# Two heads per matmul in the block means of the first batch, a wider first mixing product, a split last product, and a new order of all steps

## The chip, the cores and the metric

The kernel runs on one core of a Trainium2 chip. The metric is device time in microseconds. Before the change three runs took 621.28, 622.59 and 622.96 us; the median, 622.59 us, is the number to compare with. One more execution was taken with the hardware profiler: it took 626.52 us, and its trace spans 624.3 us from the first to the last instruction.

## What is computed

Per batch (4 batches, 8 heads of 64 dimensions, 768 positions) a local attention of window 16 that also sees 24 block summaries, and then a feed-forward layer of width 2048 on the 512 joined channels, with a low-rank mixing over positions in front of it. Cut to what matters here:

```python
k_sum = k.reshape(B, H, nb, block, D).max(axis=3)        # block = 32, nb = 24
v_sum = v.reshape(B, H, nb, block, D).mean(axis=3)
scores_all = concat([where(mask_l, q @ k.T / 8, -1e9), q @ k_sum.T / 8 + log(32)])
x = softmax(scores_all) @ concat([v, v_sum])             # heads joined: (B, S, 512)
u = x + (x.T @ U @ V).T                                  # U: (768, 32), V: (32, 768)
out = u + relu(u @ w_ch1) @ w_ch2                        # (512, 2048), (2048, 512)
```

## The kernel before

Everything is written as small steps with short names, and a table, `PLAN`, lists the steps in the order in which they are recorded; each engine carries its own instructions out in that order. The part up to the first slash is the attention of batch 0 and its way into the feed-forward layer (names with a leading dot); every later slash is a place between two groups of products of the layer, into which steps of later batches are put. Nothing else sets the order, so a step that waits holds all that stands behind it on its engine.

**Batch 0** is called the head here. Its steps are: loads of keys, queries and value pairs (`.lk`, `.lq`, `.lv`, lines 310, 324, 345, all on SP's queue, each waiting until the load eight places ahead of it has landed), block maxima and their spreading (`.K`, `.Kp`, `.Kd`, lines 418 and 433), scores (`.S`, line 474), mask and exponentials on DVE and ACT (`.E`, lines 499 and 509), transposes (`.T`, line 583), copies of them (`.C`, line 589), the product with the values (`.V`, line 599), the normalising (`.N`, line 629). Block means of the values are made by TensorE: `block_means` (`.M0`, `.M1`, line 399) multiplies a 32-column selection matrix with the values of one head, 65 columns with the column of ones. Four heads go to the four groups of 32 output partitions, and the loop over the heads is the inner one, so that matmuls next to each other write to different groups: 48 matmuls for four heads. `block_means_out` (`.Mo`, line 411) copies the result to `vsum`, and `value_summaries` (`.Bp`, `.Dp`, ..., line 437) puts it into each head's values, which `.V` reads.

The mixing of batch 0 is `mix_t` (`.I`, line 642; two tiles of 128 channels at a time), `mix_s` (`.J`, line 660) and `mix_u` (`.G`, lines 676 and 684: three transposes and the product that adds the mixed rows). Then come the products of the feed-forward layer, `up` (line 1015, 12 matmuls of 384 columns) and `down_rows` (line 1037, nine of 512) in turn. Matmuls of no use (`keep_busy`, `.w4`, line 1139, four of 120 columns each) stand where TensorE would have nothing to do.

**Batches 1 to 3** have their attention spread over the products of the batch before. Batch 3 ends with `second_phase` (line 1498): sums of products of 384 columns, each added to the rows that are kept (line 1524) and sent (line 1529).

Float32 matmuls show as two records in the trace, each with a weight load; the products of the layer show as one.

Of the kernel before, what the change touches and what calls it, by code (L numbers as in the profile page):

```python
# [18 lines left out]
P = 128  # L19
# [16 lines left out]
VALS = 8  # L36
# [31 lines left out]
    .lu .li .X .w4 .z1 .w4 .lk0 .lk3 .K0 .Xt0 .Kd0 .lq0 .lm .lq3 .lk2 .K3 .S0 .Kd3 .S3 .m .K2  # L68
    .Kp2 .E0.2 .w4 .lq2 .E0.1 .lk1 .F .w4 .lq1 .E1.0 .E7.0 .E6.2 .E1.1 .lv0 .S2 .lv1 .E0.0 .E1.2
    .T1 .K1 .E7.2 .Xt1 .T0 .E7.1 .C0 .E6.1 .lk7 .C1 .E5.2 .E5.0 .E6.0 .Kp1 .E5.1 .lk6 .w4 .T7  # L70
    .S1 .T5 .Xt2 .E2.0 .E4.1 .E2.1 .lq7 .T6 .E3.0 .lq6 .lq4 .M0 .E3.2 .E2.2 .E3.1 .Mo0 .Dp0
    .E4.0 .lk4 .K7 .Kp7 .lk5 .T2 .Bp1 .T3 .C6 .E4.2 .C5 .K6 .Bp0 .C7 .S7 .Kd6 .V1 .C2 .lv2 .T4
    .Dp3 .Xs .Bp3 .V0 .V7 .K4 .E15.2 .lq5 .Kp4 .Dp2 .E14.2 .E15.1 .V6 .C3 .N3 .E15.0 .E14.1 .lv3
    .S6 .Xl .C4 .la0 .S4 .K5 .Qs .E14.0 .Bd2 .Dp1 .E8.1 .V5 .E13.0 l1.0.0 .Kp5 .V4 .E8.2 .N0 .S5
    .E12.2 .E8.0 .V3 .V2 .E11.1 .E13.1 .E12.0 .M1 .lr .E9.0 .E12.1 .E11.2 .T12 .E13.2 .E11.0
    .E9.1 .T8 .T15 .Mo1 .Z0 .C12 .C15 .Dp6 .E10.2 .E10.1 .la1 .Qf .E10.0 .N1 .N2 .T13 .lb0 .T14
    .I0 .Y0.0 .T11 .E9.2 .Bd6 .Dd5 .T9 .Io0 .C11 .Bp4 .Bp7 .C13 .la2 .C8 .Y0.1 .Dp4 .V12 .lb1
    .C9 .V11 .V13 .Y0.2 .J0 .lb2 .V8 .N6 .la4 .Bp5 .T10 a1.0.0 .la3 .V9 .C14 .V14 .Jo0 .C10 q1.0
    .V10 .Dp7 .N4 k1.0 .G0.0 .V15 .G0.1 .lb3 .N5 .Z1 .N7 .Go0.0 a1.0.0 .G1.1 .Go0.1 .I2 .G1.0
    .Y1.0 .Io2 .J2 .z0 .w4 .Y1.1 .Jo2 .G0.2 .W0 .G0.3 .Y1.2 .Go0.2 l1.0.1 .Go0.3 .Z2 .G1.2  # L80
    .Go1.1 .Go1.2 a1.0.0 t2 W0.5 .G1.3 a1.0.0 .Go1.0 t2 .Go1.3 .U0.0 .W1 a1.0.0 / / / t2 c0.4 t2
    t2 a1.0.0 K1.0 .lb4 t2 c0.3 t3 a1.0.0 a1.0.1 w0.0 c1.2 / l1.1.0 w0.1 / x1.1 t3 x0.2 t3 v1.1
    D1 Ka1.0 v1.0 / c1.3 k1.1 S1.0.1 / E1.0.1.0 E1.0.1.1 W0.6 E1.0.1.2 S1.0.0 t3 a1.0.1 t4
    E1.0.0.1 t3 c0.5 E1.0.0.0 D0 K1.1 t5 a1.0.1 E1.0.0.2 a1.0.1 t3 Ka1.1 x0.3 w1.0 / T1.0 x1.2
    q1.1 k1.2 K1.2 / / c1.4 S1.1.0 a1.0.1 t4 / E1.1.0.2 W1.5 U0 S1.1.1 E1.1.0.0 a1.1.0 E1.1.0.1
    W1.6 s1.0 Ka1.2 q1.2 U1 w1.1 E1.1.1.2 E1.1.1.0 t4 a1.0.1 D2 E1.1.1.1 t4 k1.3 Us0 t4 t4 t5 t5
    Us1 f1.0 / c1.5 U4 a1.0.1 a1.0.1 x1.3 / D3 x0.4 a1.0.1 c0.6 / W0.7 t6 S1.2.0 t5 Ba1.1.1 U3
    T1.1 W0.8 E1.2.0.1 Ba1.0.0 E1.2.0.0 a1.1.0 E1.2.0.2 / t5 s1.1 t5 / q1.3 x0.5 W1.7 t6 x1.4
    a1.1.0 D4 S1.2.1 W0.9 Ba1.0.1 E1.2.1.1 K1.3 f1.1 E1.2.1.2 / E1.2.1.0 t6 / t6 c0.7 c0.8 P1.0
    Ba1.1.0 t6 / c1.6 W1.8 N1.0 T1.2 w2.0 t7 Ka1.3 t8 k1.4 / S1.3.0 / s1.2 E1.3.0.2 E1.3.0.0  # L90
    S1.3.1 t6 E1.3.0.1 q1.4 c1.7 P1.1 w2.1 k1.5 x1.5 E1.3.1.0 E1.3.1.1 t7 v1.2 E1.3.1.2 N1.1
# [36 lines left out]
    q2.6 E2.5.0.1 f2.3 h1.2 / / F P2.3 R2.0 K2.6 a2.1.1 / / d1.1 v2.4 p0 p1 K2.7 a2.1.1 q2.7 p1
    h1.3 s2.4 Kd2.6 / / a2.1.1 F y1.2 / E2.5.1.2 p0 d2.0 p1 p0 / E2.5.1.1 / N2.3 / / R2.1
    Ba2.4.1 Ba2.4.0 F Ds0 E2.5.1.0 Ds1 / v2.5 h1.4 f2.4 / / k3.0 y1.3 p1 S2.6 T2.5 s2.5 p0  # L130
    E2.6.1.1 E2.6.0.1 / / p0 E2.6.1.2 / r2.1 E2.6.0.0 Kd2.7 E2.6.1.0 / E2.6.0.2 a3.0.0 h1.5 r2.0
    p1 Ba2.5.1 / y1.4 K3.0 P2.4 d3.0 f2.5 v2.6 M2.0 d2.1 / N2.4 Mo2.0 / / y1.5 d3.1 T2.6 h1.6 /
    p0 / / / F a3.0.0 / S2.7 / Ba2.5.0 E2.7.0.0 E2.7.0.2 E2.7.1.0 Ba2.6.0 E2.7.1.1 g2.0 E2.7.1.2
    / / y1.6 d4.0 / / E2.7.0.1 / d4.1 / J2.0 Jo2.0 s2.6 P2.5 / p1 h1.7 Ds2 T2.7 g2.1 y1.7 /
    a3.0.0 / F k3.2 / Ds4 h1.8 p0 d5.0 p0 O2.0.1 N2.5 O2.0.1 p0 v2.7 / d5.1 K3.2 f2.6 y1.8 / F
    Ds5 O2.0.2 / O2.0.0 h1.9 / Ba2.6.1 / / y1.9 / F / / O2.0.2 h1.10 / p1 Kd3.2 O2.0.1 R2.2 /
    d7.0 P2.6 Ba2.7.0 a3.0.0 l3.0.1 s2.7 / / / p0 Kd3.0 r2.2 / / p1 / / p1 y1.10 / O2.0.3 / / p0
    p0 d6.0 h1.11 y1.11 d6.1 q3.0 Ba2.7.1 O2.0.1 h1.12 p1 / f2.7 / / / a3.0.1 P2.7 a3.0.0 O2.0.2
    / y1.12 O2.0.1 / / N2.6 / p1 O2.0.3 N2.7 p1 R2.3 Ds3 p0 M2.2 O2.0.1 O2.0.2 / / / / d7.1 g2.2
    h1.13 / / Mo2.2 O2.0.3 J2.2 O2.0.3 O2.0.3 p0 O2.0.2 O2.0.2 / / y1.13 F p1 Ds6 p0 r2.3 a3.0.1  # L140
# [50 lines left out]
def body(ctx: ExitStack, tc, q0, q1, k, v, vn, uv, w1, w2, mask, ident, rep, out):  # L191
# [1290 lines left out]
    def second_phase(st):  # L1482

        banks = {}
        for i in range(8 * len(OPS)):
# [20 lines left out]
            if q == 3:  # L1506
                second_out(st, i, n, c, ps)
# [157 lines left out]
```

## Time and profile before

| | |
|---|---|
| median of 3 runs | 622.59 us |
| profiled execution, its own time | 626.52 us |
| its span | 624.3 us |
| TensorE busy | 610.4 us (98%) |
| VectorE, ScalarE, GpSimd busy | 446.5, 350.9, 345.6 us |
| SP's DMA queue | 147.38 MB |

TensorE is the engine to look at: it is busy for nearly all of the span. The granted clock column shows 1.00 in every stretch but the last. What remains is to see where TensorE waits, and which of its work is needed.

### The profile page before, as it was taken

The numbers are of one execution on the slowest core, as the hardware profiler recorded it, in microseconds if no ns is written. First come the engines' busy times: TensorE is split into PE (matmuls) and PEld (weight loads), VectorE is DVE, ScalarE is ACT, GpSimd is POOL, SyncE is SP. The second block draws the span as 40 slices with busy tenths as digits, with TensorE's granted clock in tenths as the row PEclk, the third lists the DMA queues.
The fourth block names the chain that finished last, engine by engine and source line by source line (L and its number), as shares of the span: only waits on it lengthen the run. The fifth ranks groups of instructions, "written<-read, shape, count | busy, mean of one in ns | idle before, by whom it ended". The sixth has DMA issues, their size and how long they took to land.

```text
span 624.3 us, 14694 instructions
## 1 busy us (share of the span) xinstructions
PE 610.4 (98%) x5376; PEld 557.9 (89%) x5376; DVE 446.5 (72%) x1139; ACT 350.9 (56%) x794; POOL 345.6 (55%) x393
## 2 busy tenths in 40 slices
PE   7899999999999999999999999999999999999997
PEld 6679989889987999988887899998888899999997
DVE  5689768678888766779787764776557553579992
ACT  3776666563653666665544556675463556767620
POOL 5377964786666687785345677654333575640000
PEclk9999999999999999999999999999999999999999
DMA  8997998999968678799896786687879645455443
GB/s 222 230 323 246 285 313 258 288 291 325 295 197 281 226 239 262 241 301 300 262 305 181 210 266 203 198 256 237 253 242 311 220 133 168 149 191 203 145 119 126
DMA packets 97559, 148.30 MB, mean 238 GB/s; under 512 B 9680, under 2 KB 67920, under 8 KB 97488
## 3 DMA queue, kind: packets, MB, share of 16 engines
q1 hardware_dynamic: 97488, 147.38, 76.4%
q8 instruction: 42, 0.69, 0.5%
q14 instruction: 29, 0.24, 0.1%
HBM read 104.67 MB, written 42.66 MB: 236 GB/s over the span
## 4 chain that ended last, share of the span: by engine, by line
PE 81%; DMA 12%; SPq 3%; DVE 1%; issue 1%; ACT 1%; POOL 1%; DVEq 0%; ACTq 0%
PE ps_h L1300 25%; PE acc L1396 17%; PE ps_h L1015 10%; PE acc L1037 10%; PE accx L1498 4%; PE accy L1498 3%; PE accz L1498 3%; DMA place<-in_k 2%; PE ps_x L613 2%; DMA dsum<-tmp 2%; PE ps_s L474 2%; PE ps_s L451 2%; DMA there<-squares 2%; SPq L542 1%; DMA whole<-up 1%; DMA place<-in_v 1%
## 5 line engine op out<-in xcount | busy, mean ns | idle before, releaser
L967 POOL TENSOR_TENSOR parts<-whole,parts 128x512 fp32r<-128x512 f32 (+1 forms) x128 | 159.3, 1258 | 77.3 <-ACT parts L963 72.9
L1300 PE MATMUL ps_h<-place,parts 128*128 128x384 f32 x1008 | 179.5, 336 | 0.7 <-DVE x L629 0.7
L1300 PEld LDWEIGHTS ps_h<-place,parts 128*128 128x128 f32 x1008 | 174.3, 188 | 3.0 <-PE ps_h L1300 1.0
L1396 PE MATMUL acc<-gh,parts 128*128 128x256 f32 (+1 forms) x512 | 133.6, 341 | 0.0
L1396 PEld LDWEIGHTS acc<-gh,parts 128*128 128x128 f32 x512 | 88.6, 189 | 12.3 <-issue 1.4
L963 ACT CAST parts<-whole 128x512 fp32r<-128x512 f32 (+1 forms) x144 | 80.8, 581 | 11.9 <-issue 4.6
L1396 PE MATMUL acc<-gl,parts 128*128 128x512 f32 (+1 forms) x256 | 86.5, 338 | 0.0
L1015 PE MATMUL ps_h<-place 128*128 128x384 f32 x384 | 73.9, 341 | 0.4 <-DVE x L695 0.3
L509 ACT ACTIVATE e<-e,neg 128x120 f32<-128x120 f32 x144 | 52.0, 390 | 33.4 <-DVE neg L499 32.3
L1015 PEld LDWEIGHTS ps_h<-place 128*128 128x128 f32 x384 | 67.2, 188 | 3.1 <-DVE x L695 0.7
L1037 PE MATMUL acc<-place,gh 128*128 128x512 f32 x192 | 66.5, 400 | 0.0
L1369 ACT ACTIVATE gh<-place 128x768 fp32r<-128x768 f32 x32 | 27.1, 846 | 62.2 <-PE acc L1396 62.2
L264 POOL TENSOR_SCALAR val<-place 128x512 f32<-128x512 f32 (+1 forms) x33 | 54.1, 1642 | 9.4 <-ACT place L244 4.4
L289 POOL TENSOR_TENSOR place<-val,place 128x512 fp32r<-128x512 f32 x29 | 37.6, 1301 | 29.7 <-ACT place L288 25.2
L1374 DVE SCALAR_TENSOR_TENSOR gl<-place,gh 128x768 fp32r<-128x768 f32 x32 | 38.3, 1196 | 20.3 <-ACT gh L1369 20.2
L1396 PEld LDWEIGHTS acc<-gl,parts 128*128 128x128 f32 x256 | 48.5, 189 | 4.5 <-DVE gl L1374 0.2
L743 POOL TENSOR_TENSOR place<-tmp,place 128x384 fp32r<-128x384 f32 x24 | 27.8, 1163 | 41.0 <-ACT place L739 34.2
L1037 PEld LDWEIGHTS acc<-place,gh 128*128 128x128 f32 x192 | 36.1, 188 | 7.4 <-ACT gh L1027 0.2
L499 DVE CUSTOM_DVE_ANT_0 e<-ps_s,mask_sb 128x120 f32<-128x120 f32 x144 | 35.1, 276 | 6.2 <-PE ps_s L451 4.1
L1027 ACT ACTIVATE gh<-ps_h 128x384 fp32r<-128x384 f32 x32 | 15.7, 489 | 41.0 <-PE ps_h L1015 40.9
L1037 PE MATMUL acc<-place,gl 128*128 128x512 f32 x96 | 37.7, 393 | 0.0
L1329 DVE TENSOR_TENSOR place<-place,ps_h 128x384 f32<-128x384 f32 x24 | 13.3, 554 | 28.7 <-PE ps_h L1300 28.6
(153 smaller groups left out, 1043.4 us busy)
## 6 DMA issues: line engine op xcount, KB each, us to landing
place<-in_w SPq DMA_DIRECT2D x32, 512.0 KB, 5.8
whole<-up SPq DMA_DIRECT2D x24, 512.0 KB, 4.8
there<-squares SPq DMA_DIRECT2D x24, 384.0 KB, 4.8
at<-there SPq DMA_DIRECT2D x96, 96.0 KB, 3.4
whole<-up SPq DMA_DIRECT2D x24, 384.0 KB, 3.9
whole<-down SPq DMA_DIRECT2D x16, 512.0 KB, 5.6
vt<-in_v SPq DMA_DIRECT2D x48, 146.2 KB, 4.2
kt<-in_k SPq DMA_DIRECT2D x24, 288.0 KB, 4.8
```

The lines of the kernel that those rows point to most:

```text
L264: nc.gpsimd.tensor_scalar(f32(bits), f32(hi), 0.0, None, ALU.mult)
L289: engine.tensor_tensor(lo, val, f32(hi), ALU.subtract)
L499: nc.vector.tensor_tensor_reduce(out=e[:, u, :], in0=ps[:, i * KC : (i + 1) * KC], in1=mask_sb[:, m, :], scale=-SCALE, scalar=BIG, op0=ALU ...
L509: nc.scalar.activation(e[:, u, :], e[:, u, :], AF.Exp, bias=st.neg[h][:, u : u + 1], scale=-1.0,)
L963: nc.scalar.copy(hi, whole)
L967: (nc.vector if key[0] == "second" else nc.gpsimd).tensor_tensor(lo, whole, f32(hi), ALU.subtract)
L1015: nc.tensor.matmul(ps[:, :NH], w_split[0, f][:, c % 2, part_w, c // 2], ut[c], start=(n == 0), stop=(n == 3 * NC - 1),)
L1037: nc.tensor.matmul(acc[t], gt[:, sl], w_split[1, f][:, part_w], start=(first and j == 0), stop=(last and j == 2),)
L1300: nc.tensor.matmul(ps, a[:, sa, i], b[i][:, sb], start=(first and n == 0), stop=(n == 5), skip_group_check=not first,)
L1374: nc.vector.scalar_tensor_tensor(gl, h, 0.0, f32(gh), ALU.max, ALU.subtract)
L1396: nc.tensor.matmul(place, w[:, part_w, c * P : (c + 1) * P], gt[:, q0:q1], start=(f == 0 and i == 0 and j == 0), stop=(f == NF - 1 and j = ...
L1498: nc.tensor.matmul(ps, w[j][:, sa, c * P : (c + 1) * P], gate[sb], start=fresh and q == 0 and j == 0 and k == 0, stop=q == 3 and j == 1 an ...
```

## The change

- `block_means` takes two heads per matmul: 130 columns in place of 65, 24 matmuls for four heads, in two steps (`.M0.0`, `.M0.1`). Each step fills one group of 32 output partitions with 12 matmuls in a row; groups 2 and 3 are not used. `block_means_out` copies the two halves one after the other.
- `mix_t` of batch 0 mixes 256 channels per matmul where it does two tiles at once, and the channel tiles 2 and 3 are now mixed one by one (`.i2`, `.i3`, `.j2`, `.j3`).
- `mix_u` of batch 0 is taken apart into transposes (`.G`) and the added product (`.g`), and `up` into four steps by channel tile (`.u`), so that products of the layer can start on the first channel tile.
- The last accumulation of `second_phase` is made in two column parts, 256 and 128, each added and sent by itself.
- The matmuls of no use are 512 columns wide and stand in other places (six in place of 24).
- `PLAN` is another order throughout.

```diff
-    .T1 .K1 .E7.2 .Xt1 .T0 .E7.1 .C0 .E6.1 .lk7 .C1 .E5.2 .E5.0 .E6.0 .Kp1 .E5.1 .lk6 .w4 .T7
+    .lq4 .T2 .E7.0 .lk4 .C2 .E5.2 .T0 .E6.2 .C1 .M0.0 .M0.1 .E5.1 .Xt2 .E7.2 .lk7 .E3.1 .C4
...
-    def block_means(st, g):
-
-        ps = bank("ps_n")
+    def block_means(st, g, j):
+
+        if g not in st.ps_n:
+            st.ps_n[g] = bank("ps_n")
+        ps = st.ps_n[g]
         for u, t in itertools.product(range(NU), range(2)):
             i, n = u % 2, NB - 2 - (t * 12 + ORDER.index(u) * 2)
             rows = KC if i else W
-            for j in range(4):
-                nc.tensor.matmul(
-                    ps[32 * j : 32 * j + 32, :DV],
-                    means_w[:rows, i, n : n + 32],
-                    st.vt[4 * g + j][i][:rows, (u // 2) * 2 + t],
...
+            nc.tensor.matmul(
+                ps[32 * j : 32 * j + 32, : 2 * DV],
+                means_w[:rows, i, n : n + 32],
+                vt0[2 * g + j][i][:rows, :, (u // 2) * 2 + t],
...
     def block_means_out(st, g):
         st.vsum[g] = small.tile([P, DV], F32, name="vsum")
-        nc.scalar.copy(st.vsum[g], st.ps_n.pop(g)[:, :DV])
+        ps = st.ps_n.pop(g)
+        for i in range(2):
+            nc.scalar.copy(st.vsum[g][64 * i : 64 * i + 64], ps[:64, i * DV : (i + 1) * DV])
...
     def mix_t(st, c, n):
 
         ps = bank("ps_m")
-        for i in range(n):
+        w = n if st.b == 0 else 1
+        for i in range(0, n, w):
             for s in range(NU):
                 g = (s + 2 * i) % 4
                 nc.tensor.matmul(
-                    ps[R * g : R * g + R, i * P : (i + 1) * P],
+                    ps[R * g : R * g + R, i * P : (i + w) * P],
...
         for _ in range(n):
-            nc.tensor.matmul(ps[:, :KC], spin, spin[:, :KC], start=True, stop=True)
+            nc.tensor.matmul(ps, spin[:, :P], spin, start=True, stop=True)
...
+            for u0, u1 in ((0, 2), (2, 3)) if last else ((0, 3),):
+                part = slice(u0 * P, u1 * P)
```

The order around the block means of heads 0 to 3, on TensorE; `ps_s` are scores, `ps_t` transposes, `ps_w` matmuls of no use, `ps_n` the block means, `ps_x` products with the values. Before:

```order
L1139 MATMUL ps_w<-kt 128x120 x4
L583 MATMUL ps_t<-ident_sb,gl 120x128 x3
L474 MATMUL ps_s<-place,x 64x120 x12
L583 MATMUL ps_t<-ident_sb,gh 120x128 x3
L583 MATMUL ps_t<-ident_sb,gl 120x128 x3
L399 MATMUL ps_n<-place,means_w 32x65 x48
L583 MATMUL ps_t<-ident_sb,gl 120x128 x6
L474 MATMUL ps_s<-place,x 64x120 x12
L599 MATMUL ps_x<-place 64x65 x6
```

Now:

```order
L594 MATMUL ps_t<-ident_sb,gh 120x128 x3
L1168 MATMUL ps_w<-kt 128x512
L594 MATMUL ps_t<-ident_sb,gh 120x128 x3
L594 MATMUL ps_t<-ident_sb,gl 120x128 x3
L594 MATMUL ps_t<-ident_sb,gh 120x128 x3
L407 MATMUL ps_n<-place,means_w 32x130 x24
L594 MATMUL ps_t<-ident_sb,gh 120x128 x3
L485 MATMUL ps_s<-place,x 64x120 x24
L594 MATMUL ps_t<-ident_sb,gl 120x128 x6
L610 MATMUL ps_x<-place 64x65 x6
```

The four scores of heads 0 to 3 still stand ahead of the block means and those of heads 4 to 7 behind them; one group of transposes has moved behind.

Around the block means of heads 4 to 7, on TensorE; `ps_m` and `ps_r` are the mixing. Before:

```order
L599 MATMUL ps_x<-place 64x65 x12
L399 MATMUL ps_n<-place,means_w 32x65 x48
L583 MATMUL ps_t<-ident_sb,gh 120x128 x6
L583 MATMUL ps_t<-ident_sb,gl 120x128 x3
L583 MATMUL ps_t<-ident_sb,gh 120x128 x3
L583 MATMUL ps_t<-ident_sb,gl 120x128 x3
L642 MATMUL ps_m<-x,u_sb 32x128 x12
```

Now:

```order
L610 MATMUL ps_x<-place 64x65 x24
L407 MATMUL ps_n<-place,means_w 32x130 x24
L594 MATMUL ps_t<-ident_sb,gh 120x128 x9
L654 MATMUL ps_m<-x,u_sb 32x256 x6
L594 MATMUL ps_t<-ident_sb,gl 120x128 x3
L610 MATMUL ps_x<-place 64x65 x6
```

All eight products with the values of heads 0 to 3 stand ahead of these block means in both, and eight behind; six groups of transposes stand behind them now, where eight did.

The loads on SP's queue up to the first two value pairs. Before:

```order
L1152 DMA place<-in_uv 128x768
L1149 DMA ident_sb<-in_ident 128x128
L310 DMA place<-in_k 128x3x192 x2
L324 DMA x<-in_q 64x384 x2
L1147 DMA mask_sb<-in_mask 128x120
L324 DMA x<-in_q 64x384 x2
L310 DMA place<-in_k 128x3x192
L324 DMA x<-in_q 64x384 x2
L310 DMA place<-in_k 128x3x192
L324 DMA x<-in_q 64x384 x2
L345 DMA place<-in_v 96x780 x4
```

Now:

```order
L1183 DMA place<-in_uv 128x768
L312 DMA place<-in_k 128x3x192
L331 DMA x<-in_q 64x384 x2
L312 DMA place<-in_k 128x3x192 x3
L331 DMA x<-in_q 64x384 x4
L1178 DMA mask_sb<-in_mask 128x120
L312 DMA place<-in_k 128x3x192
L331 DMA x<-in_q 64x384 x2
L1180 DMA ident_sb<-in_ident 128x128
L352 DMA place<-in_v 96x780 x4
```

One more load of keys stands ahead of the values: five in place of four.

## Rows read from the trace of the kernel before

**Rows 1.** The head of the page and its first part: span, busy time and share of each engine.

```profile
span 624.3 us, 14694 instructions
PE 610.4 (98%) x5376; PEld 557.9 (89%) x5376; DVE 446.5 (72%) x1139; ACT 350.9 (56%) x794; POOL 345.6 (55%) x393
```

**Rows 2.** Busy time of each engine by stretch of the span: us from the start, length, busy us (and records) of each engine, granted clock, DMA share, GB/s.

```profile
10.00:15.00 5.00, 5.00 (x57) 4.42 (x51) 4.68 (x32) 3.18 (x10) 1.99 (x8) 1.00 0.98 241
15.00:20.00 5.00, 4.09 (x85) 3.24 (x85) 2.69 (x23) 4.39 (x14) 0.00 (x0) 1.00 1.07 245
...
200.00:250.00 50.00, 49.66 (x342) 47.05 (x342) 34.43 (x93) 31.13 (x72) 34.84 (x47) 1.00 0.79 249
250.00:300.00 50.00, 48.89 (x589) 43.95 (x588) 40.98 (x125) 29.15 (x68) 33.41 (x41) 1.00 0.91 283
300.00:350.00 50.00, 49.17 (x442) 41.85 (x441) 37.15 (x80) 22.88 (x43) 25.56 (x25) 1.00 0.82 245
...
450.00:500.00 50.00, 49.56 (x446) 42.06 (x445) 31.06 (x55) 24.56 (x47) 20.99 (x16) 1.00 0.81 253
```

**Rows 3.** TensorE's instructions of the head in order of time: start, us, line, tile, shape, records, and the idle time before them with what ended it.

```profile
7.60 3.01 PE L474 MATMUL ps_s<-place,x 64*64 64x120 f32 x48 [2.84 <-DMA x<-in_q]
10.53 3.23 PE L1139 MATMUL ps_w<-kt 128*128 128x120 f32 x16
13.69 0.85 PE L474 MATMUL ps_s<-place,x 64*64 64x120 f32 x24
...
18.41 0.54 PE L399 MATMUL ps_n<-place,means_w 96*32 96x65 f32 x20
19.72 1.35 PE L399 MATMUL ps_n<-place,means_w 120*32 120x65 f32 x76 [0.78 <-DMA place<-in_v]
21.01 0.87 PE L583 MATMUL ps_t<-ident_sb,gl 128*120 128x128 f32 x6
22.38 1.38 PE L474 MATMUL ps_s<-place,x 64*64 64x120 f32 x24 [0.51 <-POOL place L433]
...
25.86 2.19 PE L474 MATMUL ps_s<-place,x 64*64 64x120 f32 x48
...
28.84 0.57 PE L599 MATMUL ps_x<-place 120*64 120x65 f32 x12 [0.28 <-ACT gl L509]
30.08 1.31 PE L474 MATMUL ps_s<-place,x 64*64 64x120 f32 x24 [0.67 <-DMA x<-in_q]
...
33.37 1.36 PE L399 MATMUL ps_n<-place,means_w 120*32 120x65 f32 x76 [0.43 <-DMA place<-in_v]
34.66 0.87 PE L583 MATMUL ps_t<-ident_sb,gh 128*120 128x128 f32 x6
...
36.44 0.86 PE L642 MATMUL ps_m<-x,u_sb 128*32 128x128 f32 x24
37.24 0.54 PE L583 MATMUL ps_t<-ident_sb,gl 128*120 128x128 f32 x3
...
38.54 1.16 PE L599 MATMUL ps_x<-place 120*64 120x65 f32 x33 [0.17 <-issue]
...
47.17 1.05 PE L1139 MATMUL ps_w<-kt 128*128 128x120 f32 x8
48.06 0.49 PE L676 MATMUL ps_u<-ident_sb,x 128*128 128x128 f32 x3
48.30 0.42 PE L684 MATMUL ps_u<-vm_st,t_st 128*128 128x384 f32 x1
...
54.39 0.39 PE L1037 MATMUL acc<-place,gh 128*128 128x512 f32 x1
```

**Rows 4.** One line at a time: records of its weight loads and matmuls, ns min/median/max, first and last start, forms. The block means (65 columns), the transposes and the mixing of batch 0 (128 columns), the product after it (256 columns).

```profile
L399 PE MATMUL ps_n<-place,means_w x192: 217/220/245, 18.4 to 34.5; 96*32 96x65 f32 x96, 120*32 120x65 f32 x96
L642 PE MATMUL ps_m<-x,u_sb x192: 270/273/298, 36.4 to 480.8; 128*32 128x128 f32 x192
L660 PE MATMUL ps_r<-t,rep_sb x16: 377/379/483, 39.6 to 487.6; 128*128 128x256 f32 x16
```

**Rows 5.** The chain of work that ended last, some of its pieces in order of time: start, us, what. The last load of values in the head, scores of batch 1, whole-array matmuls of 120 columns, and the last accumulation of the kernel.

```profile
25.46 7.87 DMA place<-in_v
33.33 0.04 issue
...
62.94 0.66 PE ps_s L451 x6
...
612.45 8.37 PE accy L1498 x48
620.82 0.02 issue
620.84 0.56 DVE o L1524
```

**Rows 6.** Two groups of DVE by shape, of the adding of products to kept rows: busy us, mean ns.

```profile
L1542 DVE TENSOR_TENSOR o<-acc,x 128x256 f32<-128x256 f32 x8 | 2.8, 410 | 0.0
L1524 DVE TENSOR_TENSOR o<-x,accy 128x384 f32<-128x384 f32 x4 | 2.2, 548 | 6.8 <-PE accy L1498 6.8
```

More of the change, by code (lines that the diff above doesn't have):

```diff
@@ L320, in load_q, with load_half_q @@
         st.qt[h] = qd0[h] if st.b == 0 else qz[h % 2].rearrange("p u q -> p (u q)")[:, :NH]
-        for r, src in ((0, q0[st.b, :, h]), (64, q1[st.b, :, h])):
-            flat = src.rearrange("d u q -> d (u q)")
-            i = flat.shape[1] // 2 - NH // 2
-            nc.sync.dma_start(out=st.qt[h][r : r + 64], in_=flat[:, i : i + NH])
+        for t in range(2):
+            load_half_q(st, h, t, nc.sync)
+    def load_half_q(st, h, t, by):
+        if st.b == 0:
+            st.qt[h] = qd0[h]
+        flat = (q0, q1)[t][st.b, :, h].rearrange("d u q -> d (u q)")
+        i = flat.shape[1] // 2 - NH // 2
+        by.dma_start(out=st.qt[h][64 * t : 64 * t + 64], in_=flat[:, i : i + NH])
     def load_qk(st, h):
@@ L670, in mix_s_out, with turn_tiles @@
         nc.vector.tensor_tensor(t_st[lo], ps[lo], f32(t_st)[lo], ALU.subtract)
-    def mix_u(st, hf, c):
+    def turn_tiles(st, hf, c):
         cols = slice(c * P, (c + 1) * P)
-        ps = bank("ps_u")
+        ps = st.ps_u[hf, c] = bank("ps_u")
         for i in range(3):
@@ L683, in mix_u, with add_mixed @@
             )
+    def add_mixed(st, hf, c):
         nc.tensor.matmul(
-            ps[:, :NH], st.t_st[:, c], vm_st[:, hf * NH : (hf + 1) * NH], start=False, stop=True
-        )
-        st.ps_u[hf, c] = ps
+            st.ps_u[hf, c][:, :NH],
+            st.t_st[:, c],
+            vm_st[:, hf * NH : (hf + 1) * NH],
+            start=False,
+            stop=True,
+        )
+    def mix_u(st, hf, c):
+        turn_tiles(st, hf, c)
+        add_mixed(st, hf, c)
     def add_rows(st, hf, c, kept):
@@ L1007, in store_down_sums, with up_channel @@
             )
-    def up(st, hf, f):
-        uh, ul = st.u[hf]
-        ps = bank("ps_h")
-        n = 0
-        for part_w, ut in ((0, uh), (0, ul), (1, uh)):
-            for c in range(NC):
-                nc.tensor.matmul(
-                    ps[:, :NH],
-                    w_split[0, f][:, c % 2, part_w, c // 2],
-                    ut[c],
-                    start=(n == 0),
-                    stop=(n == 3 * NC - 1),
-                )
-                n += 1
-        return ps
+    begun = {}
+    def up_channel(st, f, hf, c):
+        uh, ul = st.u[hf]
+        if c == 0:
+            begun[f, hf] = [bank("ps_h"), 0]
+        ps, done = begun[f, hf]
+        assert done == c
+        begun[f, hf][1] = c + 1
+        for n, (part_w, ut) in enumerate(((0, uh), (0, ul), (1, uh))):
+            nc.tensor.matmul(
+                ps[:, :NH],
+                w_split[0, f][:, c % 2, part_w, c // 2],
+                ut[c],
+                start=(c == 0 and n == 0),
+                stop=(c == NC - 1 and n == 2),
+            )
+    def up(st, hf, f):
+        for c in range(begun.get((f, hf), (None, 0))[1], NC):
+            up_channel(st, f, hf, c)
+        return begun[f, hf][0]
     def up_out(ps):
@@ L1185, in body @@
         "Jo": lambda c: mix_s_out(st, c, 2),
-        "G": lambda hf, c: mix_u(st, hf, c),
+        "G": lambda hf, c: turn_tiles(st, hf, c),
+        "g": lambda hf, c: add_mixed(st, hf, c),
         "Go": lambda hf, c: mix_u_out(st, hf, c),
@@ L1494, in second_phase @@
             ps = banks[to, c]
-            for j in range(2):
-                gate = st.gates[2 * g + j]
-                for k, (sa, sb) in enumerate(((0, 0), (0, 1), (1, 0))):
-                    nc.tensor.matmul(
-                        ps,
-                        w[j][:, sa, c * P : (c + 1) * P],
-                        gate[sb],
-                        start=fresh and q == 0 and j == 0 and k == 0,
-                        stop=q == 3 and j == 1 and k == 2,
-                        skip_group_check=not fresh,
-                    )
-            if q == 3:
-                second_out(st, i, n, c, ps)
+            last = i == 8 * len(OPS) - 1
+            last_to = n == len(OPS) - 1 and c == 1
+            for u0, u1 in ((0, 2), (2, 3)) if last else ((0, 3),):
+                part = slice(u0 * P, u1 * P)
+                for j in range(2):
+                    gate = st.gates[2 * g + j]
+                    for k, (sa, sb) in enumerate(((0, 0), (0, 1), (1, 0))):
+                        nc.tensor.matmul(
+                            ps[:, part],
+                            w[j][:, sa, c * P : (c + 1) * P],
+                            gate[sb][:, part],
+                            start=fresh and q == 0 and j == 0 and k == 0,
+                            stop=(q == 3 or last_to and q == 2) and j == 1 and k == 2 or last,
+                            skip_group_check=last or not fresh,
+                        )
+                if q == 3:
+                    second_out(st, i, n, c, ps, u0, u1)
             yield
```

268 lines of the change are left out of this document (139 added, 129 removed).

## The prediction, on record before the changed kernel ran

> **What bounds the kernel now.** I read the page first: TensorE is busy for 610.4 us of a span of 624.3 [rows 1], so the kernel is nearly a list of TensorE's work, and a change is worth what it takes from that list or from TensorE's waits. The busy time by stretch then shows where the waits are. Behind the head there is little: 0.34, 1.11, 0.83 and 0.44 us in the four worst stretches, 2.7 us together [rows 2]. The rest is in the head and the last 4 us. The order of time on TensorE shows the head: before 18.4 us it waits or makes matmuls of no use; from the block means on it is short of time. Between 18.41 and the first `down_rows` at 54.39 its waits are 0.78, 0.51, 0.28, 0.67, 0.43 and 0.17 us [rows 3]. The chain that ended last says what holds the second block means: the last value load, issued at 25.46, landed at 33.33 [rows 5]. Behind that, TensorE works through 21.0 us (33.37 to 54.39) with almost no gap. So matmul time added behind the first block means is paid, apart from the waits that it fills.
>
> **Block means, the first term.** Before, 76 records took 1.29 us (33.37 to 34.66), 17 ns each; the 96 of a full set, fed without a wait, are 1.6 us. One record of 65 columns lasts 220 ns, of 128 columns 273, of 256 columns 379 [rows 4]: 53 ns for 63 columns more, 106 for 128 more, so about 0.83 ns a column, and 65 columns occupy what they pass through for some 55 ns. Seventeen ns a record is possible only because four groups of outputs were fed in turn (4 x 17 = 68 ns per group).
>
> Now each of two steps puts 12 matmuls, 24 records of 130 columns, one after another into one group. No row shows matmuls in a row for one and the same 32-column group, so I bound it. High end: they follow each other like matmuls that fill the whole array. Such scores of batch 1, 120 columns, took 0.66 us for six records, 110 ns each [rows 5]; ten columns more make 119 ns, and 48 records 5.7 us. Low end, if the second step runs beside the first as the four groups did: half, 2.9 us. I take 5.7, because the row with consecutive matmuls on the same output columns is the nearest. The set then costs 4.1 us more, twice. The Trainium skill (TensorE: Matmul & The Clock Gate, Part 3: Packing small matmuls — row/col tiling) has matmuls start and end strictly in program order, and run together only on different tiles; by that rule the 12 of one step cannot pass each other, the sum below stands, and with the low end it would be 0.5 us instead of 6.1. No row here shows it either way.
>
> **Up to the second block means.** The first set waited for values (0.78 us) and ended at 21.01 [rows 3]. In the new queue five key loads stand ahead of these values instead of four: 288 KB more at 241 to 245 GB/s [rows 2] is 1.2 us. The first step now also reads the pair loaded second. It starts at 19.7 + 1.2 = 20.9 and ends at 26.6, **5.6 us later**.
>
> Between the two sets three groups of transposes are added (nine groups stood elsewhere; five took 1.78 us from 34.66 to 36.44, 0.36 each): 1.1 us. A matmul of no use, 2 x 512 columns, adds 0.9 us: **+2.0**. Against it the waits of this stretch go, since the data will be there: 0.51 + 0.28 + 0.67 + 0.43 = 1.9 us. The four scores in it were slow too, held inside by their operands: 1.38 + 2.19 + 1.31 us against 0.85 for each of the four undisturbed [rows 3], 1.5 us: together **-3.4**. The second set starts at 33.4 + 5.6 + 2.0 - 3.4 = 37.6, and the values, even if they land 1 or 2 us later than 33.3, are no longer the bound. What is late next is TensorE itself. ScalarE's copy `.Mo`, and behind it GpSimd's summaries and the products with the values, wait with it; there are transposes and mixing to fill that.
>
> **Behind it.** Second set +4.1; two groups of transposes fewer, -0.7; the matmuls of no use at 47.17 (0.89 us to 48.06) gone, -0.9; a wait of 0.17 filled, -0.2. Mixing: 24 records took 0.80 us (36.44 to 37.24); six matmuls of 256 columns over four groups give two groups four records each, 4 x 0.22 = 0.9, and the two single tiles make 2 x 4 records of 128 columns, 0.9 where 0.8 stood: +0.2. Taking `mix_u` and `up` apart moves the same matmuls about; no cost. Two scores of batch 1 (0.66 each) come into the head and are missing behind it: nothing. Together **+2.5**.
>
> **The end.** The last accumulation makes 48 records in 8.37 us [rows 5], 174 ns each, six of them 1.05. Three transposes of 128 columns stand 0.24 us apart from what follows (48.06 to 48.30, [rows 3]), 80 ns each; taking 256 columns halfway, at 127, the split costs 6 x 127 + 6 x 80 = 1.24, 0.2 more. The last addition, 0.548 us for 384 columns and 0.410 for 256 [rows 6], falls to 0.27: -0.3. **-0.1**; a shorter last transfer may give up to 0.3 more, which no row prices, and nothing less than zero.
>
> **The rest.** The loop behind the head keeps its matmuls. Its 2.7 us of waits come from engines that now get 6 us more of a lead; but the new order can set waits of its own. Between -2.7 and +2 I take **-0.5**.
>
> **Sum:** 5.6 + 2.0 - 3.4 + 2.5 - 0.1 - 0.5 = **+6.1 us**, 1.0%. On the profiled execution that is a span of 630.4. That execution lies 3.9 us over the median of the runs; the difference carries over, so 622.6 + 6.1 = **628.7 us**. What a measurement of this kernel can tell from no change is 0.3%, 1.9 us: faster is below 620.7, slower above 624.5.
>
> **Rivals.** *Two groups overlap* (each set 2.9 us). First set to 23.8, 2.8 later; second at 33.4 + 2.8 + 2.0 - 3.4 = 34.8; behind it 1.3 instead of 4.1, so -0.3; with the end and the rest +0.5: **623.1**, no change. For it: four groups did overlap. Against: the two steps stand behind each other, not in turn.
>
> *Faster: a record costs the same whatever its columns.* If the 17 ns were the cost of issuing a record, a set would be 48 x 17 = 0.8 us. The first ends at 21.7. The second cannot start before its values: 33.4. Behind it -0.8 - 0.7 - 0.9 - 0.2 + 0.2 = -2.4, and -0.6 for the end and the rest: **619.6**. It decides where the 48 records stand closer than some 30 ns. For it: 68 ns a group is 13 more than the columns account for. Against: 0.83 ns a column in three shapes [rows 4]. The Trainium skill (TensorEngine Tiling (Array Packing), Instruction Overhead) speaks for fewer matmuls: about 60 cycles go into each beside its columns, so an estimate by that page is 48 x 25 ns = 1.2 us spared per set. By rows only some 10 ns a record stand beside the columns.
>
> *Slower still: the first set at half rate.* Sixteen records of 120 columns from 10.53 took 3.16 us, 198 ns each, after TensorE had stood idle 2.84 us to 7.60; eight of the same at 47.17 took 0.89, 111 each [rows 3]. The granted clock column says 1.00 in the stretch of the first [rows 2], but the durations stand two to one, as 1.2 and 2.4 GHz would. In the new order only four groups of transposes and one matmul of no use stand between the scores and 20.9, so TensorE will idle there again. If the whole first set ran so, it would be 5.7 us more: **634.4**; a part of that is as likely as all.
>
> **Chances.** Forecast 0.58, two groups 0.16, cost by record 0.13, half rate 0.13. The forecast's own range, with the filled waits at 2 to 4.5 us and the loop at -2.7 to +2, is 625.5 to 632. To hold 8 in 10 I go from 620.5, which cuts half of the faster case, to 632.5, which cuts most of the half-rate one. Faster: 0.12 of the cost by record, 0.02 of the two groups, 0.02 of the forecast: 0.16. Same: 0.13 of the two groups, 0.04 of the forecast, 0.01: 0.18. Slower: the rest, 0.66.
>
> **What would show it.** In the new trace the block means' records should stand 110 to 125 ns apart, two sets of 5 to 6 us, each with about twice 12 matmuls in a row; the second set should start at 36 to 39 us without a wait for values; the first `down_rows` should come 6 to 8 us later than 54.39, 1.3 us of it scores of batch 1 that are missing later. I am wrong if the records of a set stand 60 ns apart or closer, if the first `down_rows` comes before 57, or if the loop behind the head loses or gains more than 3 us of waits.

## Result and the profile after

The changed kernel takes **629.47 us** (median of 4 runs, 627.61 to 630.61); beside it the kernel before took 622.78 (4 runs, 621.28 to 623.59). The ratio is **1.0107, interval 1.0076 to 1.0139**: 6.7 us slower, by more than the 0.3% that can be told apart. The forecast was 6.1 us and 628.7. The profiled execution took 629.66 us with a span of 627.9, so it is a typical one; that of before lay 3.9 us above its median. The two spans are only 3.6 us apart, and that is what two traces can account for.

The head of the page, first part (compare [rows 1]):

```profile
span 627.9 us, 14435 instructions
PE 614.8 (98%) x5240; PEld 556.8 (89%) x5240; DVE 436.7 (70%) x1141; ACT 350.9 (56%) x798; POOL 343.0 (55%) x393
```

TensorE has 136 matmul records fewer and is busy 4.4 us longer. The stretches of [rows 2] (us, length, then busy us and records of each engine, granted clock, DMA share, GB/s):

```profile
10.00:15.00 5.00, 2.92 (x72) 2.24 (x72) 4.71 (x33) 2.27 (x7) 3.03 (x11) 1.00 0.95 258
200.00:250.00 50.00, 50.00 (x343) 47.26 (x342) 33.95 (x93) 29.55 (x69) 38.85 (x51) 1.00 0.81 246
250.00:300.00 50.00, 48.13 (x520) 43.74 (x519) 37.55 (x121) 29.18 (x67) 29.26 (x38) 1.00 0.92 278
300.00:350.00 50.00, 49.72 (x512) 42.31 (x511) 38.39 (x90) 23.65 (x47) 20.25 (x19) 1.00 0.82 242
450.00:500.00 50.00, 50.00 (x449) 43.05 (x448) 29.10 (x56) 25.70 (x50) 20.72 (x16) 1.00 0.91 269
```

The four stretches of the loop have 2.15 us of waits where they had 2.72: in this execution the loop is as it was. The head in order of time on TensorE (columns as in [rows 3]):

```profile
15.50 0.54 PE L594 MATMUL ps_t<-ident_sb,gh 128*120 128x128 f32 x3 [1.73 <-ACT gh L520]
...
18.08 5.15 PE L407 MATMUL ps_n<-place,means_w 96*32 96x130 f32 x48
23.16 0.55 PE L594 MATMUL ps_t<-ident_sb,gh 128*120 128x128 f32 x3
...
33.88 5.15 PE L407 MATMUL ps_n<-place,means_w 96*32 96x130 f32 x48
38.96 1.20 PE L594 MATMUL ps_t<-ident_sb,gh 128*120 128x128 f32 x9
...
54.45 0.83 PE L462 MATMUL ps_s<-kt,qz 128*128 128x120 f32 x6
...
57.40 0.82 PE L462 MATMUL ps_s<-kt,qz 128*128 128x120 f32 x6
...
59.03 0.39 PE L1066 MATMUL acc<-place,gh 128*128 128x512 f32 x1
```

Each set occupies 5.08 us (18.08 to 23.16, 33.88 to 38.96), 106 ns a record, where a full set before is 1.6. Neither waits for values. The first `down_rows` comes at 59.03, 4.6 us later than the 54.39 of [rows 3], 1.3 of it the scores of batch 1 at 54.45 and 57.40. One record's own duration, by its line (ns min/median/max; compare the first of [rows 4]):

```profile
L407 PE MATMUL ps_n<-place,means_w x96: 272/273/299, 18.1 to 38.8; 96*32 96x130 f32 x48, 120*32 120x130 f32 x48
```

The values' loads on SP's queue, in order of time:

```profile
9.69 0.58 SPq L1180 DMA_DIRECT2D ident_sb<-in_ident  x1
10.32 1.84 SPq L352 DMA_DIRECT2D place<-in_v  x4
12.20 0.43 SPq L312 DMA_DIRECT2D place<-in_k  x1
```

One line of the same view of the kernel before, for its first four value loads:

```profile
9.59 1.99 SPq L345 DMA_DIRECT2D place<-in_v  x4
```

And the last 4 us, DVE and the queue (compare 620.84 in [rows 5] and the second of [rows 6]):

```profile
622.73 0.55 DVE L1565 TENSOR_TENSOR o<-x,accy 128x384 f32<-128x384 f32 x1 [5.46 <-PE accy L1539]
623.32 2.00 SPq L1570 DMA_DIRECT2D out_t<-o  x3
624.06 0.62 DVE L1565 TENSOR_TENSOR o<-x,accy 128x256 f32<-128x256 f32 x2 [0.78 <-PE accy L1539]
```

The addition ahead of these two stands here in the kernel before:

```profile
619.80 0.55 DVE L1524 TENSOR_TENSOR o<-x,accy 128x384 f32<-128x384 f32 x1 [6.29 <-PE accy L1498]
```

Both parts' additions start in one piece at 624.06, when the last matmul is done; the first part does not go ahead. `second_phase` records the matmuls of both parts in its last step and only notes the additions, which are recorded behind them (`finish_late`). From the addition ahead to these are 1.33 us, against 1.04 before (620.84 - 619.80): the last matmuls take 0.29 us longer. From there to the end of the span are 3.84 us, against 3.46 before (624.3 - 620.84).

### The profile page after: what moved, and what is told of

It is laid out like the page before. It is cut to its first block, busy times and chain, and to the rows that moved or that the text cites. A ratio compares the mean times of both kernels' runs of the same rounds, so it can differ in the third digit from the quotient of the medians.

```text
span 627.9 us, 14435 instructions
## 1 busy us (share of the span) xinstructions
PE 614.8 (98%) x5240; PEld 556.8 (89%) x5240; DVE 436.7 (70%) x1141; ACT 350.9 (56%) x798; POOL 343.0 (55%) x393
## 4 chain that ended last, share of the span: by engine, by line
PE 84%; DMA 4%; DVE 4%; issue 3%; POOL 2%; ACT 2%; SPq 1%; DVEq 0%; POOLq 0%
PE ps_h L1337 27%; PE acc L1433 16%; PE acc L1066 9%; PE ps_h L1041 9%; PE accx L1539 4%; DMA kt<-in_k 3%; PE accy L1539 3%; PE accz L1539 3%; PE ps_x L624 3%; PE ps_s L485 2%; PE ps_n L407 2%; PE ps_s L462 1%; POOL parts L988 1%; PE ps_x L610 1%; PE ps_t L594 1%
## 5 line engine op out<-in xcount | busy, mean ns | idle before, releaser
L1411 DVE SCALAR_TENSOR_TENSOR gl<-place,gh 128x768 fp32r<-128x768 f32 x32 | 32.3, 1009 | 16.0 <-ACT gh L1406 15.9
L1057 DVE SCALAR_TENSOR_TENSOR gl<-ps_h,gh 128x384 fp32r<-128x384 f32 x32 | 17.8, 555 | 26.1 <-ACT gh L1056 25.7
```

What stands on the lines that cost most here:

```text
L1411: nc.vector.scalar_tensor_tensor(gl, h, 0.0, f32(gh), ALU.max, ALU.subtract)
```

## Experiments

Three groups of runs (e1 to e4; e5 to e8, on another chip; e9 to e12), each with its own runs of the kernel before beside it; ratios are to those. A ratio is not the quotient of the two medians, and can differ from it by 0.25 points, 1.6 us. "Means" are the block means, "loop" the part of `PLAN` behind the first slash.

| run | head and means | loop | last product | us (runs) | before beside it | ratio, interval |
|---|---|---|---|---|---|---|
| e1 | new head, old means | new | split | 626.06 (12) | 624.75 (31) | 1.0023, 1.0004 to 1.0042 |
| e2 | two groups in turn | new | split | 627.23 (12) | same | 1.0034, 1.0013 to 1.0055 |
| e3 | 65 columns, group by group | new | split | 629.45 (6) | same | 1.0067, 1.0040 to 1.0095 |
| e4 | old head, new means | old | whole | 630.01 (12) | same | 1.0065, 1.0036 to 1.0095 |
| e5 | the change | new | split | 631.30 (6) | 625.47 (23) | 1.0118, 1.0087 to 1.0148 |
| e7 | old head, old means | new | whole | 629.38 (12) | same | 1.0075, 1.0043 to 1.0108 |
| e8 | new head, old means | new | whole | 626.90 (12) | same | 1.0042, 1.0007 to 1.0077 |
| e9 | new head, new means | old | split | 628.90 (12) | 624.57 (35) | 1.0077, 1.0045 to 1.0109 |
| e10 | new head, old means | old | whole | 624.46 (12) | same | 0.9984, 0.9956 to 1.0012 |
| e11 | e1 again | new | split | 628.17 (12) | same | 1.0055, 1.0026 to 1.0085 |
| e12 | the change | new | split | 629.71 (12) | same | 1.0075, 1.0046 to 1.0103 |

e6 is one more profile of the kernel before.

**e1, the block means as before.** The edit, with the one copy of 128 rows that goes with it:

```diff
-            nc.tensor.matmul(
-                ps[32 * j : 32 * j + 32, : 2 * DV],
...
-                vt0[2 * g + j][i][:rows, :, (u // 2) * 2 + t],
...
+            for j in range(4):
+                nc.tensor.matmul(
+                    ps[32 * j : 32 * j + 32, :DV],
...
+                    st.vt[4 * g + j][i][:rows, (u // 2) * 2 + t],
```

> The changed kernel with the block means of before (one head per matmul, 48 matmuls of 65 columns, four groups of outputs in turn) at the places of the new order. If the loss is the block means (theory): a set falls from 5.1 us to 1.3 to 1.6, twice 3.5 us of TensorE's time go, some waits come back, and the time falls by 4 to 7 us, to 622.5 to 625.5. If the loss is the new order (rival): sets shorter, but waits for loads and exponentials take their place, and the time stays at 628 to 630.

**e2, two groups in turn.** Still 130 columns and 24 matmuls a set, but the loop over the two groups is the inner one:

```diff
         for u, t in itertools.product(range(NU), range(2)):
...
+            for j in range(2):
+                nc.tensor.matmul(
```

> The changed kernel with the same 24 matmuls of 130 columns per set, but fed to the two groups of outputs in turn instead of 12 and then 12. If matmuls on different groups run beside each other and those in a row on one group do not (theory): 48 records at about 55 ns, a set of 2.6 to 2.9 us, 2.3 us less per set, the time 624.5 to 627.5. If a matmul of 130 columns costs 106 ns a record wherever it goes (rival): sets stay at 5.1 us and the time at 628 to 631.

**e3, narrow, group by group.** The 48 matmuls of 65 columns of before, with the 12 of a head standing in a row:

```diff
-        for u, t in itertools.product(range(NU), range(2)):
+        for j, u, t in itertools.product((2 * part, 2 * part + 1), range(NU), range(2)):
```

> The changed kernel with 48 matmuls of 65 columns per set as before, but all 12 of one head after each other into one group, then the next head. If standing in a row on one group is what costs (theory): 96 records at 55 to 68 ns, a set of 5.2 to 6.5 us, the time 629 to 632, like the change. If the width of 130 columns costs (rival): 17 ns a record, a set of 1.6 us, the time 622 to 625.

What the first set became, TensorE in order of time. In e1:

```profile
18.06 1.60 PE L408 MATMUL ps_n<-place,means_w 96*32 96x65 f32 x96
...
53.89 0.39 PE L1064 MATMUL acc<-place,gh 128*128 128x512 f32 x1
```

In e2:

```profile
19.19 2.88 PE L410 MATMUL ps_n<-place,means_w 96*32 96x130 f32 x48
...
55.64 0.39 PE L1069 MATMUL acc<-place,gh 128*128 128x512 f32 x1
```

In e3:

```profile
19.17 5.11 PE L408 MATMUL ps_n<-place,means_w 96*32 96x65 f32 x96
...
60.02 0.39 PE L1063 MATMUL acc<-place,gh 128*128 128x512 f32 x1
```

This settles the block means' own price. Four groups in turn: 96 records in 1.60 us, 17 ns apart. Two in turn: 48 in 2.88, 60 ns. One: 53 ns for 65 columns (e3) and 106 for 130 (the change), 0.82 ns a column at either width. Twice as many matmuls and weight loads of half the width take the same 5.1 us, so it is neither the width nor the count but standing in a row in one group. The first `down_rows` follows: 53.89 (e1), 55.64 (e2), 59.03 (the change), 60.02 (e3). In e2 and e3 the first set itself starts 1.1 us later than in the other two; their granted clock from 10 to 15 us is 0.79 and 0.72, where the other two have 1.00. Counted from the start of the first set, the four are 35.83, 36.45, 40.95 and 40.85 us. The times follow less plainly: e1 is 0.23% above before and e2 0.34%, e3 0.67%, but e1 once more (e11, below) is 0.55% above. e2 and e3 came out as expected; e1 at 626.06 lies 0.6 us above its range.

**e4, the block means alone, in the kernel before.** The new `block_means`, its copies, and in `PLAN`:

```diff
-    .S1 .T5 .Xt2 .E2.0 .E4.1 .E2.1 .lq7 .T6 .E3.0 .lq6 .lq4 .M0 .E3.2 .E2.2 .E3.1 .Mo0 .Dp0
+    .S1 .T5 .Xt2 .E2.0 .E4.1 .E2.1 .lq7 .T6 .E3.0 .lq6 .lq4 .M0.0 .M0.1 .E3.2 .E2.2 .E3.1 .Mo0 .Dp0
```

> The kernel before, in its own order, with nothing but the new block means (two heads per matmul, one step after the other). If the block means are the loss (theory): two sets of 5.1 us instead of 1.3 to 1.6, 7.2 us more, of which waits of up to 3.4 us between the sets take a part: 626 to 630. If the order is the loss (rival): 622 to 624.

TensorE in order of time:

```profile
18.99 5.15 PE L400 MATMUL ps_n<-place,means_w 96*32 96x130 f32 x48
...
35.08 5.15 PE L400 MATMUL ps_n<-place,means_w 96*32 96x130 f32 x48
...
59.22 0.39 PE L1041 MATMUL acc<-place,gh 128*128 128x512 f32 x1
```

Nothing else is changed here, and the first `down_rows` comes 4.8 us later than in [rows 3]; the ratio says 0.65%, 4.1 us (2.2 to 5.9). The block means alone cost that much in the old order.

**e5, the change again,** with no edit, beside e6 to e8.

> The changed kernel itself once more, beside the others of this call. If the block means at 5.1 us a set make two thirds of the loss (theory): 4.5 to 7 us over the kernel before, and 3 to 5 over the kernel with the block means as before.

5.8 us slower than the runs of before beside it by the medians (7.4 by the ratio), with its first `down_rows` at 58.98: the result holds.

**e6, the kernel before, one more profile.**

> The kernel before, for a second profile. The first one lay 3.7 us over the median of its runs. If that was the loop behind the head (theory): the first down_rows stands again at 54 to 55 us, and the time from there to the last matmul falls from 566.4 to 562 to 565. If it was the head: first down_rows at 51 to 53.

It took 628.16 us with a span of 624.9, again above its median, so it did not show a typical execution. Busy time by stretch, granted clock third from the end:

```profile
20.00:30.00 10.00, 9.33 (x183) 7.49 (x183) 4.48 (x21) 4.13 (x13) 5.33 (x15) 0.66 0.86 207
```

The clock was lower for a while in the head, the first set waited 2.30 us for its values (0.78 in [rows 3]), the first `down_rows` came at 56.35 in place of the 54 to 55 expected, and the loop had 1.95 us of waits (540 - 538.05). The question it was to answer stays undecided.

**e7, the change's loop order behind the head of before.** Head, block means and last product as before; only the part of `PLAN` behind the head is the change's (the few steps of batch 1 that the change has in its head stand at the start of the loop):

```diff
-    .Go1.1 .Go1.2 a1.0.0 t2 W0.5 .G1.3 a1.0.0 .Go1.0 t2 .Go1.3 .U0.0 .W1 a1.0.0 / / / t2 c0.4 t2
+    .Go1.1 .Go1.2 a1.0.0 t2 W0.5 .G1.3 a1.0.0 .Go1.0 t2 .Go1.3 .U0.0 .W1 a1.0.0 /  / t2 K1.0
...
```

> The kernel before with its own head (steps up to the first slash), its own block means and last product, and the loop steps in the order of the change; the few steps of batch 1 that the new order has ahead of the loop stand at its start. If the new order of the loop costs some 2 to 3 us (theory, from what is left between the times when the block means are undone): 2 to 4 us over the kernel before. If the loops are worth the same (rival): within 1.5 us of it.

The loop order alone costs 0.75%, 4.7 us (2.7 to 6.8). TensorE's waits from 60 to 600 us, by what was waited for (us in total, times, longest):

```profile
PE ps_x L615 <- DMA at<-there: 3.6, 3, 1.4
PE ps_h L1017 <- DVE gl L1030: 1.5, 1, 1.5
PE acc L1398 <- DVE neg L501: 1.1, 1, 1.1
```

and the same stretch's busy time:

```profile
60.00:600.00 540.00, 533.11 (x4421) 487.86 (x4420) 379.70 (x926) 310.57 (x689) 312.12 (x325) 1.00 0.79 239
```

6.9 us of waits against 3.1 in the profile of before and 1.95 in e6. More than half stand before products with the values that wait for a transfer. From the first `down_rows` to the last matmul it is 8.1 us against 3.1, e7 first and then before, and TensorE's busy time is nearly the same; so in this profile the loss is waits:

```profile
54.07:626.19 572.12, 564.03 (x4597) 517.75 (x4596) 399.74 (x969) 316.81 (x703) 314.21 (x329) 1.00 0.77 234
```

```profile
54.39:620.82 566.43, 563.32 (x4597) 517.72 (x4596) 408.35 (x969) 317.24 (x703) 315.79 (x329) 1.00 0.76 237
```

**e8, the block means, the split and the added matmul of no use undone,** with the loop of the change. Beside the edit of e1:

```diff
-            last = i == 8 * len(OPS) - 1
-            last_to = n == len(OPS) - 1 and c == 1
+            last = False
+            last_to = False
```

> The changed kernel with the block means as before, the last product in one part, and without the matmul of no use between the two sets of block means. The last part should take 3.5 us from the last matmul to the end instead of 3.85, the last matmuls 0.2 less, and the matmul of no use 0.9, unless a wait takes its place: 0.5 to 1.5 us under the kernel with the block means as before alone, so within 1.5 us of the kernel before. If it lies 2 us or more under the kernel before, the new head is worth what its trace shows (1.8 us).

626.90 us, 1.4 above before: what is left of the change is the new head and the loop order, and it still costs 0.42% (0.07 to 0.77). The split is undone here, and all profiles together price it: between the last two starts of additions to `accy` lie 1.33 us in all eight split kernels and 1.04 or 1.05 in all six whole ones, so the split costs 0.3 by its matmuls. The time behind the last matmul is not its doing: from the last addition's start to the end it is 3.45 to 3.50 us in all five profiles with the old loop, e9 with the split among them, and 3.77 to 3.89 in those with the new loop, e7 without the split among them, except 3.51 in e8. What sets it is not shown. e5 and, by the medians, e7 (3.9 us) and e8 came out as expected.

**e9, the change with the loop order of before.** Head, means and split are the change's:

```diff
-    .g0.3 a1.0.0 S1.0.1 a1.0.0 .g1.3 .Go1.1 t2 .Go0.2 .u0.0.2 l1.0.1 k1.2 .Go1.2 .Go0.3 .Y1.2
+    .g0.3 a1.0.0 a1.0.0 .g1.3 .Go1.1 t2 .Go0.2 .u0.0.2 l1.0.1 .Go1.2 .Go0.3 .Y1.2 .u0.1.1 .Go1.3
...
```

> The changed kernel with its own head (block means of two heads included; three steps of batch 1, two scores and a load of keys, stay in the loop) and its own last product, but with the loop steps in the order of before. If the new order of the loop costs some 3 us also behind the late head of the change (theory): 2 to 5 us under the change of this call, 2 to 5 over the kernel before. If a late head hides the waits of the new loop (rival): within 1.5 us of the change.

**e10, the new head alone:** e8 with that same old loop.

> The same head and the loop of before, but the block means as before, the last product in one part, and no matmul of no use between the two sets: what the experiments leave of the change as useful. If head and loop add up (theory): the head starts the products some 2 us earlier and nothing is lost behind it, so 1 to 3 us under the kernel before. If the earlier head only runs into waits of the loop (rival): within 1 us of the kernel before.

**e11 and e12, e1 and the change once more,** beside these two.

> The changed kernel with the block means as before once more, beside the change on the same chip. Theory: 3 to 6 us under the change, 1 to 3 over the kernel before.

> The changed kernel beside the other three on one chip: 5 to 8 us over the kernel before.

e12 came out as expected. e9 and e10 did as their rivals said, and e11 missed: it is 1.5 us under the change and 3.6 over before. In this last group of runs the old loop gains nothing for the change: 1.0077 (e9) and 1.0075 (e12). With the old means it does matter: 0.9984 (e10) and 1.0055 (e11), intervals that do not touch, though e11 also has the split and the matmul of no use that e10 lacks. The kernel that differs from e10 in the loop alone is e8, 1.0042 in the group before: 0.58 points, 3.6 us.

Seen the other way, undoing the block means together with the split and one matmul of no use gives 4.4 us behind the old loop (e9 to e10) and the same 4.4 behind the new one (e5 to e8, 631.30 to 626.90). The block means alone, behind the new loop, give 3.4 us in the first group (e3, whose sets cost as much as the change's, to e1) and 1.5 in the last (e12 to e11). So it is not shown that the new loop takes back part of what cheaper block means win.

TensorE's waits between 60 and 600 us (540 less its busy time) over all profiles, by where the head ends, the first `down_rows` before 57 us or after 58.7:

| | early head | late head |
|---|---|---|
| old loop | before 3.1, e6 1.95, e10 4.1 | e4 3.55, e9 0.7 |
| new loop | e1 3.1, e7 6.9, e8 7.5, e11 5.2 (e2, at 55.64: 3.9) | after 3.2, e3 2.7, e5 2.9, e12 5.1 |

The row of e7 stands above. This is what stands at the head of the waits of e11:

```profile
PE ps_x L622 <- DMA at<-there: 1.9, 2, 1.4
PE ps_u L711 <- DVE x L714: 1.8, 1, 1.8
```

The means of the four fields are 3.1 and 2.1 us with the old loop, 5.3 and 3.5 with the new one. So the new loop waits more. Behind a late head either loop waits less on the average, as it would if part of what an earlier head wins were given back there. Single profiles spread by as much as these differences (3.1 in e1 and 5.2 in e11, the same kernel), so this is a direction and no size. e10's head is earlier than before's (first `down_rows` at 53.17, not 54.39), and it is not measurably faster. e12's own profile is of its slowest execution, a span of 631.7, the first set only at 20.74 after a stretch at a granted clock of 0.67.

## Why the prediction came out

The time was right (629.5 for 628.7, in the range, on the side forecast). Its largest cause, the block means, was right and nearly right in size. That the sum came so close is luck: the first set's later start was 3.4 us too dear, the loop and the end some 4 too cheap, and they cancelled.

- **Block means: right in cause, 0.6 us a set too dear.** 5.08 us a set for 5.7 forecast, 106 ns a record for 119 (promised: 110 to 125; set of 5 to 6). The high bound went by scores that fill the array, 110 ns for 120 columns [rows 5]; the right price was the columns' own, the 0.83 ns of [rows 4] times 130, 108. By the Trainium skill (TensorE: Matmul & The Clock Gate, Part 3: Packing small matmuls — row/col tiling) matmuls on different tiles of the array run at the same time, and start and end in program order; e1 to e3 agree: records stand 17, 60 and 53 ns apart with four, two and one group (65, 130 and 65 columns).
- **The first set's later start: wrong.** The step said 1.2 us more of key loads stand ahead of the values, so the set starts at 20.9. It started at 18.08 without a wait, 1.6 us earlier than the resumed set of [rows 3]: the values' issue began at 10.32, 0.7 us later than before (9.59), and they had landed in time. The step took the 241 to 245 GB/s of 10 to 20 us for the price of the added load, but ahead of the values the new queue carries more in the same time: from 5 to 10 us 275 to 305 GB/s in all ten profiles with the new head, 220 to 263 in the four with the old. Besides, the 19.7 that it added to was the start in one execution. The same head waited 2.30 us for these values in e6 and not at all in e7:

```profile
20.35 1.35 PE L399 MATMUL ps_n<-place,means_w 120*32 120x65 f32 x76 [2.30 <-DMA place<-in_v]
```

```profile
17.98 1.59 PE L401 MATMUL ps_n<-place,means_w 96*32 96x65 f32 x96
```

The first ten microseconds of the profile after, in the columns of [rows 2]:

```profile
0.00:5.00 5.00, 3.69 (x5) 1.61 (x6) 0.08 (x1) 1.83 (x2) 3.60 (x10) 1.00 0.62 182
5.00:10.00 5.00, 3.79 (x29) 1.30 (x27) 1.85 (x4) 0.00 (x0) 1.08 (x5) 1.00 1.03 305
```

and of before:

```profile
0.00:5.00 5.00, 3.77 (x16) 3.49 (x16) 0.00 (x0) 1.84 (x2) 4.30 (x13) 1.00 0.58 162
5.00:10.00 5.00, 2.40 (x44) 2.38 (x47) 2.75 (x11) 0.00 (x0) 2.11 (x7) 1.00 1.02 263
```

20 and 42 GB/s more over 5 us each are 310 KB, the added load of 288. The first set ended 2.15 us later (23.16 for 21.01), not 5.6.
- **Between the sets: right.** 12.36 us (21.01 to 33.37) became 10.72 (23.16 to 33.88), -1.6 for -1.4. The second set started without a wait for values, as promised, but at 33.88 and not at 36 to 39, since the first had ended earlier.
- **Behind the second set: right.** From its start to the first `down_rows` 21.02 us became 25.15: +4.1, of which 1.3 are the moved scores, for 2.5 + 1.3. The first `down_rows` thus came 4.6 later, short of the 6 to 8 promised; without the scores 3.3.
- **The end: wrong in sign.** -0.1 forecast, +0.7 in the profiles: the last matmuls +0.29 for the 0.2 forecast, and +0.38 behind them (3.84 for 3.46) for -0.3, which by the profiles of e7 and e9 goes with the loop order and not with the split. The addition of the first part should have run beside the second part's matmuls. It waited for the last of them, so the split only added work.
- **The loop: mis-sized.** -0.5 forecast, bounded by -2.7 and +2. In the two profiles it is indeed about level. But e7 measured +4.7 for the new order behind the old head, and e8 against e10 has it cost 3.6 behind the new head with the old means. Behind the change's own late head e9 against e12 has it cost 0.8, inside the noise. Head and end give 3.3 + 0.7 of the 6.7 us; the other 2.7 would be the loop's by subtraction, and since before's own profile was not of a typical execution, that remainder is not shown row by row.

Of the rivals, two groups overlapping fell (5.08 us, not 2.9; e2 is that case built, with 2.88). Cost by record fell: 130 columns take twice what 65 do. The Trainium skill (TensorEngine Tiling (Array Packing), Instruction Overhead) gives each matmul an overhead of about 60 cycles, and one of a single column the latency of one of 60; e3 shows nothing beside the columns, 96 records of 65 columns at 53 ns, which is the columns at 0.82 ns. Half rate did not come for a set: every set of 130 columns in one group took 5.15 us or less, in e12 too, where the granted clock had been 0.50, the lower of its two levels, 1.2 GHz, from 15 to 20 us, just ahead of it.

**Open:** which step of the new loop order sets the waits (no run moved single steps); and how far the two losses overlap. Behind the new loop the block means are worth 1.5 us in the last group of runs and 3.4 in the first, while e1 and the first result, from different groups of runs, are 0.84 points of ratio apart, 5.2 us.

## What to carry to other kernels

Small matmuls that write to different groups of output partitions must stand in turn: the loop over groups belongs innermost, and halving the number of matmuls is worth nothing if they then stand in a row in one group (1.60 against 5.1 us for the same sums). A new order of the next stage can lose as much as the changed stage itself (4.7 us for the loop behind the old head, 4.1 for the block means), so undo each part alone. Compare kernels that differ in one part only: one pair of runs here had the block means worth 1.5 us behind the new loop, another 3.4. An added load is not paid at the rate of the stretch in which the transfer is awaited, if the queue has room ahead of it.

## What was not expected of the hardware

- Two column parts of one accumulator were not free one by one: DVE took up both at 624.06, after the last matmul of either. Both additions are recorded behind the matmuls of both parts, so this can be the recorded order and need not be the hardware; an addition recorded between the two parts was not tried.
- Executions of one kernel on one chip scatter by 2 us and more (before in the last group of runs: 33 of 35 runs from 621.7 to 628.0). Part of it shows in TensorE's granted clock. In eight of the 14 profiles its mean over 10 to 20 or 20 to 30 us is 0.95 or less (down to 0.66 in e6 and e8, 0.67 in e12), in the other six it is 1.00 in both, and one kernel has both: the change 1.00 after and in e5, 0.67 in e12, whose first `down_rows` comes 2.7 us later (61.69 for 59.03). TensorE had been about as busy there as in the profile after (7.35 and 7.37 us of 10 to 20 us).
- Waits in the loop can cost more than their own time. In e11, whose TensorE idled for 1.8 us of 202 to 206 us, the granted clock of the next four microseconds is 0.57 in the mean, close to the lower level; in e8, where TensorE idled for 2.4 us of 316 to 320 us, it is 0.73 in these four microseconds and 0.84 in the next four. A wait does not always do that: in e7, with 6.9 us of them, the clock is 1.00 throughout the loop.

```profile
202.00:206.00 4.00, 2.19 (x12) 1.74 (x11) 1.59 (x4) 1.11 (x3) 0.00 (x0) 1.00 0.69 216
206.00:210.00 4.00, 4.00 (x12) 3.10 (x11) 3.90 (x7) 2.88 (x7) 2.29 (x2) 0.57 1.05 371
```
